# Attention and experts on one core: matrices fetched in halves on SyncE's queue, products issued per quarter and bank, transposes in place, a new order

## The chip, the cores and the metric

One core of one Trainium2 chip runs the kernel. The metric is the device time of one execution in microseconds (us). Engine names are those of the profile: PE is TensorE (PEld its weight loads), DVE is VectorE, ACT is ScalarE, POOL is GpSimd, SP is SyncE, which here only issues transfers. SPq and ACTq are the instruction streams that issue transfers from SyncE and ScalarE.

## The reference

For x of shape 4 x 11456 x 128 and 32 inducing points of 128 numbers, two attention blocks run one after the other, then a layer of 8 experts of which each token uses one.

```python
def mab(q, kv):
    s = scale * (q @ kv.transpose(0, 2, 1))
    s = s - s.max(-1, keepdims=True)
    a = np.exp(s)
    a /= a.sum(-1, keepdims=True) + 1e-09
    return a @ kv
h = mab(I, x)                      # 32 rows per batch
y = mab(x, h)                      # 11456 rows per batch
...
logits = y @ w_gate                # 8 experts
expert_idx = np.argmax(logits, axis=1)
probs = softmax(logits)
gate_w = probs[np.arange(N), expert_idx]
for e in range(E):                 # rows with expert_idx == e
    out[mask] = gate_w[mask, None] * (np.maximum(xe @ w1[e], 0.0) @ w2[e])
```

All data is float32.

## The kernel before

**Tiles.** Each of the 4 batches is cut into 4 quarters of rows, and each quarter into 6 groups of 15 blocks of 32 rows. So there are 24 tiles (k = 6b + g); one is 960 KB, 128 channels by 15 blocks by 4 quarters by 32 rows, and needs one load, one output of the same size and often a second load.

**First attention (names in the plan: LT, S1, M1, E1, T1, H).** A tile is loaded (`load_xt`, L599). `scores` (L611) multiplies it by the inducing points, four products into 32 rows of a bank each. A maximum per pair of tiles (`max1` L614, `max_spread` L637, `max_fold` L643 with `columns` L575, `max_all` L648) and an exponential on ACT (L651) follow; DVE turns the result in 32 x 32 blocks (L654, into another buffer), and 15 products (`h_sum`, L664) sum it with the tile in its other layout. That layout is loaded (`load_xn`, L602) for 10 tiles and made by 15 transposes on PE (`turn`, L622) with copies out of PSUM (`turn_out`; `copy`, L630 on ACT, L632 on DVE) for 14.

**Per batch (names hT to h4, C in the tables).** After its 6 tiles a batch has its 32 rows of h (`h_turn`, `h_norm` L686 to 688, `h_center` L697 to 699). In the second attention all rows of a batch mix nearly the same h, so one expert is picked per batch (`gate_mm`, `pick` L708 to 712), and its row number is written to memory. `fetch` (L716, L717) reads the number into a register of the issuing engine and loads that expert's two matrices, 1 MB, into the one buffer `wt`: on ACT's queue for batches 0 to 2, on SP's for batch 3. `units` (L744) multiplies h by the first matrix, three DVE steps (L749, L753, L757/758) apply the relu, `second` (L766) multiplies by the second matrix, and after a fold the 32 finished rows stand in `h4`. A margin per batch (L785 to 826) bounds where this shortcut holds; a general part after the main one redoes rows outside it, of which there are none here.

**Second attention (S2, M2, E2, LG, LV, LS, PR, C, CT, SP, W, X, V, OUT).** In 6 rounds of 4 tiles: scores with h (L611 again), maximum (L831, L832), exponential (L835), gate logits of the round (L839, L844, L856 to 887, turned back in L891), `spread` of the gate weight over the rows (four products of 32 rows, L896), `weigh` (L899), and `experts` (L903): four products, one for each quarter q, each of 32 rows of `h4` by 480 columns into a bank of its own. Four copies (`evict`, L630/632) bring the banks to an output tile, and SP stores it (L605).

**Buffers.** 18 large slots hold tiles, turned tiles and outputs; 20 of 128 x 480 hold exponentials and gate values; the 8 banks of PSUM are shared by all.

**The order.** It is written by a planner that runs when the kernel is built: `make_plan` lists the operations with ranks (tables in `PLAN`), needs and assumed durations, and `schedule` simulates the engines and at each free moment takes the ready operation of lowest rank. STICK is added to the rank of a PE operation that changes between column-tiled (C), full (F) and row-tiled (R) products. A copy may go to ACT or DVE: DVE takes it only if ACT is busy for more than BEHIND ns. For a transfer it assumes a start 1000 ns after issue (START), 420 bytes per ns in all (RATE), shared by weight between the heads of the queues (7680 for SP's tiles, 8192 for the matrices), and 360 ns to land (LANDING); at most 2 transfers of SP are in flight in the plan. On the chip every engine runs its instructions in this order, each when its semaphores allow.

Of the kernel before, what the change touches and what calls it, by code (L numbers as in the profile page):

```python
# [31 lines left out]
NCONST = 128 + 128 + 4 + 8 + 1 + 12 + 64 + 4  # L32


HOP, SAME, FREE, START, LANDING, RATE = 70, 35, 40, 1000, 360, 420
SWITCH, STICK, INFLIGHT, BEHIND = 150, 315, 2, 66
# [11 lines left out]
class Op:  # L48
    __slots__ = ("name", "rank", "dur", "fn", "deps", "take", "use", "kind", "dma", "seq", "eng", "start", "end", "left", "ready", "param")

    def __init__(self, name, rank, dur, fn, deps=(), take=(), use=(), kind="", dma=None):
# [3 lines left out]
        self.eng = self.start = self.end = None  # L55
# [4 lines left out]
class Lines:  # L60
    def __init__(self):
        self.queues, self.at = {}, 0

    def put(self, o, when, queue, size, weight):
        self.queues.setdefault(queue, []).append([when, size, weight, o])

    def shares(self, t):
        heads = [q[0] for q in self.queues.values() if q and q[0][0] <= t]
        total = sum(h[2] for h in heads)
        return [(h, RATE * h[2] // total) for h in heads]  # L70
# [7 lines left out]
    def advance(self, t):  # L78
        landed = []
        while True:  # L80
# [4 lines left out]
            for q in self.queues.values():  # L85
                if q and q[0][0] <= n and q[0][1] <= 0:
                    landed.append((n, q.pop(0)[3]))
                    if q and q[0][0] < n:
                        q[0][0] = n
        self.flow(t)  # L90
# [8 lines left out]
def schedule(ops, caps, groups):  # L99
# [12 lines left out]
    busy = dict.fromkeys(ENGINES, 0)  # L112
    lines = Lines()
    events, order, done, t = [], [], 0, 0
    kind, pe_end, cold, inflight = "", 0, COLD, 0
# [37 lines left out]
    while done < len(ops):  # L153
        for e in ENGINES:
# [11 lines left out]
            o = best[2]  # L166
            for x in o.dur:
                ready[x].remove(o)
# [4 lines left out]
            if e == "PE":  # L173
                if t - pe_end > IDLE:
# [10 lines left out]
            if o.dma:  # L185
                inflight += e == "SP"
                lines.put(o, t + START, *o.dma)
# [8 lines left out]
        for when, o in lines.advance(t):  # L196
            inflight -= o.eng == "SP"
            o.end = when + LANDING
# [1053 lines left out]
```

## Time and profile before

| | |
|---|---|
| median of 3 runs | 195.26 us (195.07 to 195.92) |
| the profiled execution, its own time | 194.98 us |
| its span, first to last instruction | 192.9 us |
| mean granted TensorE clock | 0.917 |
| busy: PE, DVE, ACT | 155.9, 129.2, 94.5 us |
| moved | 61.88 MB, mean 321 GB/s |

The span is what the trace shows; 2.1 us of the execution's own time lie outside it. A line of a group of instructions gives line, engine, operation, output and input with their shapes, and the count; a helper such as `copy` or `columns` gives its own line to all who call it. A float32 product is recorded as two. The clock is a share of full speed (2.4 GHz); it has two levels, and a value between them is a mean over a stretch. "idle before" is how long the engine had nothing to run, with the instruction or transfer that ended it.

### The profile page before, as it was taken

Reading aid. Unit: us, or ns where it says so; the run is one execution under the profiler, and the core shown is the slowest. Engines: PE = TensorE matmul, PEld = TensorE weight load, DVE = VectorE, ACT = ScalarE, POOL = GpSimd, SP = SyncE. Lnnn points to the kernel's source line nnn. Section 1 sums busy time; section 2 is a strip of 40 time slices with the busy share of each in tenths; the row PEclk is TensorE's granted clock in tenths of the full one; section 3 lists DMA queues with packets and bytes.
Section 4 is the critical chain, followed back from the end, with each engine's and each line's share of the span. In section 5 each row is a group of like instructions: output and inputs, shape, how many; then the busy total and the mean of one; then the engine's idle time right before and its main releaser. Section 6 shows DMA issues by size and latency. Waiting matters only on the chain.

```text
span 192.9 us, 5128 instructions
## 1 busy us (share of the span) xinstructions
PE 155.9 (81%) x2060; PEld 84.5 (44%) x2061; DVE 129.2 (67%) x357; ACT 94.5 (49%) x193; POOL 14.9 (8%) x78
## 2 busy tenths in 40 slices
PE   7569999698299999939999995698999489979500
PEld 6148558353157576334635321534652135624200
DVE  0163565489079899927879996279999739877600
ACT  3165553138133636915564957008686908652800
POOL 1000000020002202001300020001202000012000
PEclk9999999999879999987999999789999958975965
DMA  5999999999932903994999999960598896798990
GB/s 197 424 424 423 422 420 418 422 410 430 413 162 43 339 32 108 423 328 180 345 359 425 412 420 423 426 284 7 207 404 236 267 424 267 308 422 350 395 397 31
DMA packets 9389, 61.88 MB, mean 321 GB/s; under 512 B 1296, under 2 KB 1424, under 8 KB 8848
## 3 DMA queue, kind: packets, MB, share of 16 engines
q1 hardware_dynamic: 8640, 58.16, 76.0%
q10 hardware_dynamic: 720, 3.33, 4.2%
q8 instruction: 18, 0.29, 0.6%
q14 instruction: 11, 0.09, 0.1%
HBM read 37.89 MB, written 23.59 MB: 319 GB/s over the span
## 4 chain that ended last, share of the span: by engine, by line
PE 44%; DMA 30%; DVE 15%; issue 3%; ACTq 1%; SPq 0%; ACT 0%
DMA wt<-in_w 18%; DMA big<-in_xT 12%; PE bank L903 10%; PE bank L611 9%; PE bank L664 9%; PE bank L622 6%; PE bank L896 4%; DVE mid L899 3%; PE bank L839 2%; DVE big L632 2%; PE bank L575 2%; PE bank L744 2%; DVE mx L831 2%; DVE mid L654 2%; ACTq L716 1%
## 5 line engine op out<-in xcount | busy, mean ns | idle before, releaser
L630 ACT COPY big<-bank 128x480 f32<-128x480 f32 (+2 forms) x120 | 60.2, 570 | 56.7 <-PE bank L622 32.1
L903 PE MATMUL bank<-mid,h 32*128 32x480 f32 x192 | 34.4, 697 | 0.7 <-DVE mid L899 0.5
L611 PE MATMUL bank<-big,it_s 128*32 128x480 f32 x192 | 24.9, 578 | 4.3 <-DMA big<-in_xT 4.3
L622 PEld LDWEIGHTS bank<-csb,big 128*128 128x128 f32 x210 | 22.6, 141 | 12.7 <-issue 6.3
L622 PE MATMUL bank<-csb,big 128*128 128x128 f32 x210 | 27.3, 278 | 0.5 <-ACT mid L835 0.4
L664 PE MATMUL bank<-big,mid 128*32 128x129 f32 x720 | 25.9, 284 | 1.8 <-issue 1.7
L664 PEld LDWEIGHTS bank<-big,mid 128*32 128x32 f32 x720 | 22.7, 113 | 6.3 <-issue 3.2
L614 DVE TENSOR_REDUCE mx<-bank 128x1 f32<-128x480 f32 x24 | 15.5, 648 | 14.0 <-PE bank L611 13.7
L611 PE MATMUL bank<-big,hc 128*32 128x480 f32 x192 | 24.1, 589 | 0.3 <-ACT mid L835 0.3
L632 DVE COPY big<-bank 128x480 f32<-128x480 f32 (+2 forms) x32 | 20.1, 639 | 3.3 <-PE bank L622 1.9
L835 ACT ACTIVATE mid<-bank,nb 128x480 f32<-128x480 f32 x24 | 16.2, 674 | 12.0 <-DVE gzr L730 7.2
L903 PEld LDWEIGHTS bank<-mid,h 32*128 32x128 f32 x192 | 13.8, 210 | 16.1 <-ACT big L630 5.8
L651 ACT ACTIVATE mid<-bank,mx 128x480 f32<-128x480 f32 x24 | 15.3, 664 | 6.1 <-DVE mx L648 6.1
L654 DVE STREAM_TRANSPOSE mid<-mid 128x480 f32<-128x480 f32 x24 | 15.6, 661 | 1.5 <-ACT mid L651 1.5
L899 DVE TENSOR_TENSOR mid<-mid,bank 128x480 f32<-128x480 f32 x24 | 14.5, 643 | 2.6 <-PE bank L896 2.6
L831 DVE TENSOR_REDUCE mx<-bank 128x1 f32<-128x480 f32 x24 | 15.3, 638 | 1.2 <-PE bank L611 1.2
L744 PE MATMUL bank<-wt,hT_all 128*32 128x256 f32 x32 | 3.4, 508 | 14.5 <-DMA wt<-in_w 14.5
L749 DVE STREAM_TRANSPOSE gT<-bank 128x256 f32<-128x256 f32 x4 | 1.8, 450 | 14.9 <-PE bank L744 14.9
L896 PE MATMUL bank<-mid,sel 32*128 32x480 f32 x48 | 10.0, 743 | 1.4 <-DVE u L796 1.4
L611 PEld LDWEIGHTS bank<-big,it_s 128*32 128x32 f32 x192 | 5.3, 112 | 11.8 <-issue 4.3
L744 PEld LDWEIGHTS bank<-wt,hT_all 128*32 128x32 f32 x32 | 0.8, 124 | 17.2 <-issue 17.2
L611 PEld LDWEIGHTS bank<-big,hc 128*32 128x32 f32 x192 | 5.0, 113 | 7.7 <-issue 4.4
(95 smaller groups left out, 126.8 us busy)
## 6 DMA issues: line engine op xcount, KB each, us to landing
big<-in_xT SPq DMA_DIRECT2D x24, 960.0 KB, 11.6
out<-big SPq DMA_DIRECT2D x24, 960.0 KB, 6.1
big<-in_xn SPq DMA_DIRECT2D x10, 967.5 KB, 10.6
wt<-in_w ACTq DMA_DIRECT2D x3, 1024.0 KB, 9.0
wt<-in_w SPq DMA_DIRECT2D x1, 1024.0 KB, 6.6
csb<-in_consts ACTq DMA_DIRECT2D x1, 174.5 KB, 2.5
it_s<-in_indT SPq DMA_DIRECT2D x1, 16.0 KB, 2.3
wg_sb<-in_wg ACTq DMA_DIRECT2D x1, 4.0 KB, 5.3
```

The costliest lines, as they stand in the source:

```text
L611: self.nc.tensor.matmul(self.blk(ps[32 * q : 32 * q + 32, :GW]), lhsT=lhsT, rhs=x[:, :, q, :], start=True, stop=True)
L614: self.nc.vector.tensor_reduce(self.mx1[b][g // 2][:, g % 2 : g % 2 + 1], self.bank(fe)[:, :GW], AX.X, ALU.max)
L622: self.nc.tensor.transpose(ps[:, k * P : (k + 1) * P], x[:, k0 + k].rearrange("p q t -> p (q t)"), self.ident)
L630: self.nc.scalar.copy(dst, src)
L632: self.nc.vector.tensor_copy(dst, src)
L654: self.nc.vector.transpose(self.at(t), self.at(e))
L664: self.nc.tensor.matmul(ps[32 * j : 32 * j + 32, : P + 1], lhsT=e[:, k, :], rhs=x[:, k, :], start=(n < 4), stop=(n >= 2 * GB - 4))
L831: self.nc.vector.tensor_reduce(t, self.bank(fe)[:, :GW], AX.X, ALU.max)
L835: self.nc.scalar.activation(self.at(e), self.bank(fe)[:, :GW], AF.Exp, bias=self.nb2[k])
L896: self.nc.tensor.matmul(self.bank(s)[:, :GW], lhsT=self.sel[rows], rhs=self.at(ct)[rows], start=True, stop=True)
L899: self.nc.vector.tensor_tensor(out=self.at(e), in0=self.at(e), in1=self.bank(s)[:, :GW], op=ALU.mult)
L903: self.nc.tensor.matmul(self.bank(os_[q])[:, :GW], lhsT=self.h4[b][32 * q : 32 * q + 32, :], rhs=self.at(e)[32 * q : 32 * q + 32, :], star ...
```

## The change

- **Fetch.** All four fetches are issued by SP, each as two transfers of 512 KB: the first matrix, then the second. `units` waits for the first alone, `second` for the other too. The plan assumes 2600 ns to start and 600 to land for the first half.
- **Products.** `spread` and `experts` become one operation per tile and per quarter, each taking its own bank; the planner keeps a time for each of the four row tiles and waits for all of them when the kind changes. STICK is 7156 instead of 315, BEHIND 1821 instead of 66.
- **Copies.** Lists bind 57 copies of turned tiles and outputs to ACT and 42 to DVE.
- **Buffers.** DVE's transposes and the gate steps work in place, so 18 middle buffers do instead of 20, and there are 19 large slots instead of 18. `max_fold` writes to unused columns of the scores' bank. Several small buffers exist once or twice instead of four times.
- **Small steps.** `h_norm` sums as it multiplies; `pick` reads PSUM itself and a separate copy (`gate_out`) brings out the gate values; `max2` is cut into its two instructions; the warm-up is 3 products of 384 columns instead of 36 of 128; the inducing points and the gate matrix lie in the constants.
- **Order.** All ranks are new (numbers left out here).

```diff
...
-HOP, SAME, FREE, START, LANDING, RATE = 70, 35, 40, 1000, 360, 420
-SWITCH, STICK, INFLIGHT, BEHIND = 150, 315, 2, 66
+HOP, SAME, FREE, RATE, PAUSE, AGAIN, FIRST = 70, 35, 40, 420, 1500, 600, 330000
+SWITCH, STICK, INFLIGHT, BEHIND = 150, 7156, 2, 1821
...
+            if e == "PE":
+                clear = tiles[o.tile] if o.tile is not None and o.kind == kind else max(tiles)
+                if clear > t:
+                    busy[e] = clear
+                    heapq.heappush(events, (clear, 4, o.seq))
+                    continue
...
+                run = occ if o.tile is None else lat - 250
+                if t - max(tiles) > IDLE:
                     cold = max(cold, t + WINDOW)
                 if t < cold:
-                    occ, lat = 2 * occ, lat + occ
+                    occ, run, lat = 2 * occ, 2 * run, lat + run
                 if o.kind != kind:
-                    occ, lat = occ + SWITCH, lat + SWITCH
-                kind, pe_end = o.kind, t + occ
+                    occ, run, lat = occ + SWITCH, run + SWITCH, lat + SWITCH
+                kind = o.kind
+                if o.tile is None:
+                    tiles = [t + run] * 4
+                else:
+                    tiles[o.tile] = t + run
...
-SPW = 4
+JOIN = 1
+FETCH = ("SP", "SP", "SP", "SP")
 CAPS = {"gate": 2, "w": 1}
-GROUPS = {"mid": (20, {"e1": 5, "e1t": 4, "e2": 9, "lv": 2, "ls": 2, "ct": 3}), "bank": (8, {"fe": 4, "o": 5, "mi": 4, "sp": 4}), "big": (18, {"xt": 14, "xn": 5, "ob": 4})}
+GROUPS = {"mid": (18, {"e1": 6, "e2": 13, "lv": 4}), "bank": (8, {"fe": 6, "o": 8, "mi": 3, "sp": 3}), "big": (19, {"xt": 17, "xn": 6, "ob": 6})}
...
+    "ACT": [
+        "TE0.2", "TE10.1", "TE10.2", "TE12.1", "TE12.2", "TE13.1", "TE14.1", "TE14.3", "TE15.3", "TE16.1", "TE16.2",
+        "TE2.0", "TE4.3", "TE7.1", "TE7.2", "TE8.0", "TE9.0", "TE9.1", "TE9.2", "V0.0", "V0.1", "V0.3", "V1.0",
+        "V1.2", "V1.3", "V10.3", "V11.0", "V11.1", "V12.0", "V12.2", "V13.0", "V13.1", "V13.2", "V14.0", "V14.1",
+        "V15.1", "V15.2", "V15.3", "V17.0", "V18.0", "V18.1", "V19.0", "V19.3", "V2.3", "V20.0", "V22.0", "V3.1",
+        "V3.2", "V4.0", "V5.3", "V6.2", "V6.3", "V7.0", "V8.1", "V8.3", "V9.2", "V9.3", "h41", "h42", "h43",
+    ],
+    "DVE": [
+        "PC0", "PC2", "TE0.0", "TE0.3", "TE10.0", "TE10.3", "TE13.0", "TE13.2", "TE13.3", "TE14.0", "TE14.2",
+        "TE15.0", "TE15.1", "TE15.2", "TE16.3", "TE18.1", "TE18.2", "TE2.1", "TE2.2", "TE4.1", "TE4.2", "TE6.0",
+        "TE6.1", "TE6.3", "TE7.0", "TE8.1", "TE9.3", "V14.2", "V16.3", "V17.2", "V18.2", "V19.2", "V2.1", "V20.2",
+        "V21.0", "V21.2", "V21.3", "V22.1", "V22.2", "V22.3", "V23.0", "V23.2", "V3.0", "V8.0", "cc0", "h40",
+    ],
...
+        if name in side:
+            e = side[name]
+            dur, fn = {e: dur[e]}, lambda f=fn, e=e: f(e)
...
-                    tt = last = op(f"T1.{ku}", ("A", ku, "T1"), {"DVE": (590, 655)}, lambda e=e1_, t=e1t_: K.turn_e(e, t), [ex], take=[e1t_], use=[e1_])
+                    tt = last = op(f"T1.{ku}", ("A", ku, "T1"), {"DVE": (590, 655)}, lambda e=e1_: K.turn_e(e), [ex], use=[e1_])
                     if u == NG - 1:
...
-        a = hT = op(f"hn{b}", ("C", b, "hn"), vec(840), lambda mi=m0, b=b: K.h_norm(mi, b), [a], use=[m0])
-        a = hc = op(f"hc{b}", ("C", b, "hc"), vec(560), lambda b=b: K.h_center(b), [a])
+        a = hT = op(f"hn{b}", ("C", b, "hn"), vec(910), lambda mi=m0, b=b: K.h_norm(mi, b), [a], use=[m0])
+        a = hc = op(f"hc{b}", ("C", b, "hc"), vec(380), lambda b=b: K.h_center(b), [a])
         m0 = Buf("mi")
         a = op(f"cg{b}", ("C", b, "cg"), pe(400), lambda mi=m0, b=b: K.gate_mm(mi, b), [hc], take=[m0], kind="C")
-        a = ix = op(f"ix{b}", ("C", b, "ix"), vec(900), lambda mi=m0, b=b: K.pick(mi, b), [a], use=[m0])
+        a = ix = op(f"ix{b}", ("C", b, "ix"), vec(740), lambda mi=m0, b=b: K.pick(mi, b), [a], use=[m0])
+        cc = op(f"cc{b}", ("C", b, "gt"), {"ACT": (185, 290), "DVE": (150, 240)}, lambda e, mi=m0, b=b: K.gate_out(e, mi, b), [a], use=[m0])
         w = Buf("w")
-        if b < B - 1:
-            ga = op(f"GA{b}", ("C", b, "GA"), {"ACT": (1100, 1100)}, lambda w=w, b=b: K.fetch("ACT", w, b), [ix], take=[w], dma=("ACT", 1048576, 8192))
+        if FETCH[b] == "ACT":
+            ga = gc = op(f"GA{b}", ("C", b, "GA"), {"ACT": (1300, 1300)}, lambda w=w, b=b: K.fetch("ACT", w, b, 0, 2 * F), [ix], take=[w], dma=("ACT", 1048576, 8192, 1950, 750))
         else:
-            ga = op(f"GA{b}", ("C", b, "GA"), {"SP": (1100, 1100)}, lambda w=w, b=b: K.fetch("SP", w, b), [ix], take=[w], dma=("SP", 1048576, 8192))
-        gz = op(f"gt{b}", ("C", b, "gt"), {"POOL": (550, 600)}, lambda b=b: K.gate_turn(b), [ix])
+            ga = op(f"GA{b}", ("C", b, "GA"), {"SP": (2000, 2000)}, lambda w=w, b=b: K.fetch("SP", w, b, 0, F), [ix], take=[w], dma=("SP", 524288, 4096, 2600, 600))
+            gc = op(f"GB{b}", ("C", b, "GA"), {"SP": (450, 450)}, lambda w=w, b=b: K.fetch("SP", w, b, F, 2 * F), [ga], use=[w], dma=("SP", 524288, 4096, 1000, 600))
+        gz = op(f"gt{b}", ("C", b, "gt"), {"POOL": (550, 600)}, lambda b=b: K.gate_turn(b), [ix, cc])
...
-        a = op(f"P{b}", ("C", b, "P"), pe(430), lambda mi=m0, w=w, b=b: K.second(mi, w, b), [gl], take=[m0], use=[w], kind="C")
+        a = op(f"P{b}", ("C", b, "P"), pe(430), lambda mi=m0, w=w, b=b: K.second(mi, w, b), [gl, gc], take=[m0], use=[w], kind="C")
...
-        for u0 in range(0, n, SPW):
-            us = list(range(u0, min(u0 + SPW, n)))
-            sps = [Buf("sp") for _ in us]
-            sp = op(f"SP{ks[u0]}", ("X", ks[u0], "SP"), pe(800), lambda sps=sps, ct=ct, us=us: K.spread(sps, ct, us), [cb], take=sps, use=[ct], kind="R")
-            for u, s in zip(us, sps):
-                k, b = ks[u], bs[u]
-                ob = Buf("ob")
-                wg = op(f"W{k}", ("X", k, "W"), {"DVE": (570, 660)}, lambda s=s, e=e2[u]: K.weigh(s, e), [sp], use=[s, e2[u]])
-                os_ = [Buf("o") for _ in range(NQ)]
-                x = op(f"X{k}", ("X", k, "X"), pe(800), lambda os_=os_, e=e2[u], b=b: K.experts(os_, e, b), [wg, h4s[b]], take=[*os_, ob], use=[e2[u]], kind="R")
-                vs = []
-                for q in range(NQ):
-                    vs.append(op(f"V{k}.{q}", ("X", k, "V"), {"ACT": act(480), "DVE": dve(480)}, lambda e, o=os_[q], ob=ob, q=q: K.evict(e, o, ob, q), [x], use=[os_[q], ob]))
-                op(f"OUT{k}", ("X", k, "OUT"), {"SP": (400, 400)}, lambda ob=ob, b=b, g=k % NG: K.store(ob, b, g), vs, use=[ob], dma=("SP", BYTES, 7680))
+        for u, (k, b) in enumerate(zip(ks, bs)):
+            s, ob, os_ = Buf("sp"), Buf("ob"), [Buf("o") for _ in range(NQ)]
+            sp = op(f"SP{k}", ("X", k, "SP"), {"PE": (40, 1050)}, lambda s=s, lv=lv, u=u: K.spread(s, lv, u), [cb], take=[s], use=[lv], kind="R", tile=u)
+            wg = op(f"W{k}", ("X", k, "W"), {"DVE": (570, 660)}, lambda s=s, e=e2[u]: K.weigh(s, e), [sp], use=[s, e2[u]])
+            vs, x = [], None
+            for q in range(NQ):
+                x = op(f"X{k}.{q}", ("X", k, "X"), {"PE": (40, 1050)}, lambda o=os_[q], e=e2[u], b=b, q=q: K.experts(o, e, b, q), [wg, h4s[b], x], take=[os_[q]] if q else [os_[q], ob], use=[e2[u]], kind="R", tile=q)
+                vs.append(op(f"V{k}.{q}", ("X", k, "V"), {"ACT": act(480), "DVE": dve(480)}, lambda e, o=os_[q], ob=ob, q=q: K.evict(e, o, ob, q), [x], use=[os_[q], ob]))
+            op(f"OUT{k}", ("X", k, "OUT"), {"SP": (400, 400)}, lambda ob=ob, b=b, g=k % NG: K.store(ob, b, g), vs, use=[ob], dma=("SP", BYTES, 7680, 1000, 360))
...
-        self.load = [lambda: nc.sync.dma_start(self.it_s, indT), lambda: nc.scalar.dma_start(csb, consts), lambda: nc.scalar.dma_start(self.wg, wg)]
+        self.load = lambda: nc.scalar.dma_start(csb, consts)
...
-        for i in range(9):
-            self.columns(self.bank(mi)[:, 0:P], self.ones, self.ones)
+        for i in range(3):
+            self.nc.tensor.matmul(self.bank(mi)[:, 0:384], lhsT=self.ones, rhs=self.ones.unsqueeze(1).to_broadcast([P, 3, P]), start=True, stop=True)
...
-    def turn_e(self, e, t):
-        self.nc.vector.transpose(self.at(t), self.at(e))
-
-    def zero_pad(self, t):
-        self.nc.gpsimd.memset(self.at(t)[64:128, (GB - 1) * 32 : GB * 32], 0.0)
...
+    def gate_out(self, e, mi, b):
+        self.copy(e, self.cg[b], self.bank(mi)[:, E : 2 * E])
+
+    def fetch(self, e, w, b, lo, hi):
         engine = self.nc.scalar if e == "ACT" else self.nc.sync
-        row = engine.value_load(self.ii[b][0:1, 0:1], min_val=0, max_val=(E - 1) * P)
-        engine.dma_start(self.wt[w.slot], self.w[bass.ds(row, P), :])
+        if lo == 0:
+            self.row = engine.value_load(self.ii[b][0:1, 0:1], min_val=0, max_val=(E - 1) * P)
+        engine.dma_start(self.wt[w.slot][:, lo:hi], self.w[bass.ds(self.row, P), lo:hi])
 
...
-    def spread(self, sps, ct, us):
-        for s, u in zip(sps, us):
-            rows = slice(32 * u, 32 * u + 32)
-            self.nc.tensor.matmul(self.bank(s)[:, :GW], lhsT=self.sel[rows], rhs=self.at(ct)[rows], start=True, stop=True)
+        self.nc.vector.transpose(self.lv3(lv, n), c)
+
+    def spread(self, s, lv, u):
+        rows = slice(32 * u, 32 * u + 32)
+        self.nc.tensor.matmul(self.bank(s)[:, :GW], lhsT=self.sel[rows], rhs=self.at(lv)[rows], start=True, stop=True)
...
-    def experts(self, os_, e, b):
-        for q in range(NQ):
-            self.nc.tensor.matmul(
-                self.bank(os_[q])[:, :GW],
-                lhsT=self.h4[b][32 * q : 32 * q + 32, :],
-                rhs=self.at(e)[32 * q : 32 * q + 32, :],
-                start=True,
-                stop=True,
-            )
+    def experts(self, o, e, b, q):
+        rows = slice(32 * q, 32 * q + 32)
+        self.nc.tensor.matmul(self.bank(o)[:, :GW], lhsT=self.h4[b][rows], rhs=self.at(e)[rows], start=True, stop=True)
...
```

## Rows read from the trace of the kernel before

**Rows 1.** The page: busy us (share) xinstructions; GB/s in 40 slices of the span.
```profile
PE 155.9 (81%) x2060; PEld 84.5 (44%) x2061; DVE 129.2 (67%) x357; ACT 94.5 (49%) x193; POOL 14.9 (8%) x78
GB/s 197 424 424 423 422 420 418 422 410 430 413 162 43 339 32 108 423 328 180 345 359 425 412 420 423 426 284 7 207 404 236 267 424 267 308 422 350 395 397 31
```

**Rows 2.** Stretches: length, busy us (x) of each engine, clock, transfer share, GB/s.
```profile
52.03:55.60 3.57, 3.57 (x24) 1.10 (x24) 1.26 (x3) 0.00 (x0) 0.00 (x0) 0.58 0.79 325
55.60:80.00 24.40, 24.25 (x376) 15.99 (x376) 22.57 (x66) 13.59 (x29) 3.68 (x18) 1.00 0.44 154
...
84.90:89.50 4.60, 4.59 (x54) 2.27 (x58) 2.32 (x7) 0.59 (x2) 0.60 (x3) 0.63 0.84 314
...
122.15:127.10 4.95, 4.95 (x76) 3.36 (x76) 2.19 (x7) 0.00 (x0) 0.00 (x0) 0.66 1.01 420
127.10:150.60 23.50, 22.37 (x340) 10.51 (x336) 22.63 (x65) 15.64 (x34) 3.29 (x14) 1.00 0.56 206
...
154.85:162.00 7.15, 7.15 (x37) 3.21 (x38) 4.65 (x13) 2.45 (x6) 0.28 (x2) 0.58 0.80 335
...
170.00:183.70 13.70, 9.71 (x52) 3.97 (x50) 9.26 (x23) 6.68 (x14) 1.69 (x8) 0.75 0.94 388
183.70:192.90 9.20, 0.00 (x0) 0.00 (x0) 0.00 (x0) 0.00 (x0) 0.00 (x0) 0.56 0.52 207
```

**Rows 3.** Waits for L744: us in total, times, longest; timeline, first and last.
```profile
PE bank L744 <- DMA wt<-in_w: 14.5, 4, 4.7
...
52.03 1.08 PE L744 MATMUL bank<-wt,hT_all 128*32 128x256 f32 x8 [4.69 <-DMA wt<-in_w]
...
154.85 1.08 PE L744 MATMUL bank<-wt,hT_all 128*32 128x256 f32 x8 [3.05 <-DMA wt<-in_w]
```

**Rows 4.** The chain: start, us, what; then landings of the four fetches.
```profile
40.40 0.17 DVE ii L712
...
41.52 10.38 DMA wt<-in_w
...
146.31 0.16 DVE ii L712
...
148.14 6.58 DMA wt<-in_w
...
DMA to landing us min/median/max: 6.6/9.0/10.4
```

**Rows 5.** Issues on SP's queue, KB, median us to landing; landings of L605's stores.
```profile
big<-in_xT SPq DMA_DIRECT2D x24, 960.0 KB, 11.6
...
DMA to landing us min/median/max: 3.7/6.1/12.8
```

**Rows 6.** Timeline of PE around a row-tiled product: start, us, instructions.
```profile
109.98 0.99 PE L611 MATMUL bank<-big,it_s 128*32 128x480 f32 x8
...
110.79 0.99 PE L611 MATMUL bank<-big,hc 128*32 128x480 f32 x8
...
111.71 1.09 PE L903 MATMUL bank<-mid,h 32*128 32x480 f32 x8
...
112.72 1.01 PE L611 MATMUL bank<-big,hc 128*32 128x480 f32 x8
```

**Rows 7.** Timeline: one product that waited within itself, and four in a row.
```profile
116.04 1.62 PE L903 MATMUL bank<-mid,h 32*128 32x480 f32 x8
...
164.70 5.42 PE L903 MATMUL bank<-mid,h 32*128 32x480 f32 x32
```

**Rows 8.** Page, groups: copies out of PSUM to large tiles.
```profile
L630 ACT COPY big<-bank 128x480 f32<-128x480 f32 (+2 forms) x120 | 60.2, 570 | 56.7 <-PE bank L622 32.1
...
L632 DVE COPY big<-bank 128x480 f32<-128x480 f32 (+2 forms) x32 | 20.1, 639 | 3.3 <-PE bank L622 1.9
```

**Rows 9.** Timeline of SP: its first transfer.
```profile
0.77 0.39 SPq L513 DMA_DIRECT2D it_s<-in_indT  x1
```

More of the change, by code (lines that the diff above doesn't have):

```diff
@@ L48, with __init__ @@
 class Op:
-    __slots__ = ("name", "rank", "dur", "fn", "deps", "take", "use", "kind", "dma", "seq", "eng", "start", "end", "left", "ready", "param")
-    def __init__(self, name, rank, dur, fn, deps=(), take=(), use=(), kind="", dma=None):
+    __slots__ = ("name", "rank", "dur", "fn", "deps", "take", "use", "kind", "dma", "seq", "eng", "start", "end", "left", "ready", "param", "tile")
+    def __init__(self, name, rank, dur, fn, deps=(), take=(), use=(), kind="", dma=None, tile=None):
         self.name, self.rank, self.dur, self.fn = name, rank, dur, fn
@@ L61, in __init__, with put @@
     def __init__(self):
-        self.queues, self.at = {}, 0
-    def put(self, o, when, queue, size, weight):
-        self.queues.setdefault(queue, []).append([when, size, weight, o])
+        self.queues, self.at, self.last = {"SP": [[1000, FIRST, 7680, None, True]]}, 0, 0
+    def put(self, o, when):
+        queue, size, weight, start, _ = o.dma
+        q, when = self.queues.setdefault(queue, []), when + start
+        if queue == "SP" and not q and when - self.last > PAUSE:
+            when += AGAIN
+        q.append([when, size, weight, o, queue == "SP"])
     def shares(self, t):
-        heads = [q[0] for q in self.queues.values() if q and q[0][0] <= t]
+        heads = [q[0] for q in self.queues.values() if q and q[0][0] <= t and q[0][4]]
         total = sum(h[2] for h in heads)
@@ L89, in advance @@
                         q[0][0] = n
+                    if name == "SP":
+                        edge, self.last = True, n
+            sp = self.queues["SP"]
+            if edge or not sp or sp[0][0] > n:
+                for q in self.queues.values():
+                    if q and q[0][0] <= n:
+                        q[0][4] = True
         self.flow(t)
@@ L112, in schedule @@
     busy = dict.fromkeys(ENGINES, 0)
+    busy["SP"] = 10
     lines = Lines()
-    events, order, done, t = [], [], 0, 0
-    kind, pe_end, cold, inflight = "", 0, COLD, 0
+    events, order, done, t = [(10, 2, 0)], [], 0, 0
+    kind, tiles, cold, inflight = "", [0] * 4, COLD, 0
     def fits(o):
@@ L774, in part_out @@
     def part_out(self, e, mi, b):
-        self.copy(e, self.part[b], self.bank(mi)[:, 0:P])
+        self.copy(e, self.part[0], self.bank(mi)[:, 0:P])
     def part_fold(self, mi, b):
-        self.columns(self.bank(mi)[:, 0:P], self.fold, self.part[b])
+        self.columns(self.bank(mi)[:, 0:P], self.fold, self.part[0])
     def h4_out(self, e, mi, b):
@@ L934, in attn_moe_kernel @@
                 o.fn()
-    general_part(tc, K, xT, wg, w, out)
+    general_part(tc, K, xT, w, out)
 def blk(t):
```

210 lines of the change are left out of this document (112 added, 98 removed), and 177 rows, old and new, of the table PLAN.

## The prediction

> **What bounds the kernel now.** I began with the page's busy shares: TensorE 81% and VectorE 67% of a span of 192.9 us, with the memory traffic at up to 424 GB/s but nearly nothing in some slices [rows 1]. A mean hides where the time goes, so next came busy time and clock by stretch [rows 2]. TensorE is busy without a break in 55.6 to 80, while the transfers run at 0.44 of their share; in 127.1 to 150.6 it works 22.4 of 23.5 us at a transfer share of 0.56. In the middle of the kernel it is the order and speed of TensorE that counts, with VectorE close behind (22.6 of 24.4 and 22.6 of 23.5 us). What breaks this up is seen in the list of waits: four times TensorE stands before the product with the picked expert's first matrix (L744) for its load, 14.5 us together, 4.69 the first and 3.05 the last time [rows 3]. Behind every one of these waits the granted clock is low: 0.58, 0.63, 0.66 and 0.58 as means of stretches of 3.57, 4.60, 4.95 and 7.15 us [rows 2], a mixture of the full 2.4 GHz with the lower level, 1.2 GHz. Length times the missing share is 1.5 + 1.7 + 1.7 + 3.0 = 7.9 us. Waits and clock together: 22.4 us.
>
> **Why TensorE arrives too early.** The order is written by a planner in the kernel that assumes when a fetch lands. In the old code that is 1.0 us after the index is ready, plus the transfer (1 MB at 8192/15872 of 420 GB/s beside SyncE's queue, 4.84 us), plus 0.36: 6.2 us. The chain shows the truth for b=0: index ready at 40.57, landing at 41.52 + 10.38 = 51.90, so 11.3 us [rows 4]. That is 5.1 more than assumed, and TensorE waited 4.69 [rows 3]. For b=3, on SyncE's queue, it took from 146.47 to 154.72, 8.25 us, against 3.9 assumed with nothing ahead: 4.4 more, wait 3.05. The waits are the planner's error, less some slack.
>
> **Part by part.**
>
> *Fetch in halves on SyncE's queue, new due times.* The new code counts 2.6 us to start, 0.5 MB at 420 GB/s (1.25) and 0.6: 4.45 us, plus what the queue holds ahead. From rows: index to issue on SyncE was 1.67 us (146.47 to 148.14) [rows 4]; the quickest 960 KB store landed in 3.7 us [rows 5], of which half its 2.32 us at 424 GB/s falls away: 2.6; so 4.3 from below. From above, the b=3 fetch landed in 6.58 with a store ahead; less 1.24, plus 1.67: 7.0. I take a value near the lower end, 0.75 us over the plan each time, since the plan counts transfers ahead by itself: 3.0 of the 14.5 us stay, **-11.5 us**. Ends: all 14.5 gone; or, with as much ahead as the median load has (11.6 us to landing [rows 5], so 11.6 - 1.24 + 1.67 = 12.0, against 4.45 + two transfers of 2.32 = 9.1 planned), 2.9 us each, only -2.8. The second half is needed only after three VectorE steps on the first product; cover gone, it costs its own 1.24 us. The index read now stands at the head of SyncE's queue, so loads and stores behind it are held for that 1.67 us four times. While loads land 11.6 us after their issue several are already out, and from 55.6 to 80 the lines are half idle; I count nothing, and 6.7 us if every one of them were short.
>
> *Clock.* With waits of under 1 us the stretch behind should mostly stay at 2.4 GHz. Not all: the kernel's last working stretch, 170 to 183.7, has 0.75 with no fetch near [rows 2]. Ends 0 and -7.9; I take two thirds, **-5 us**.
>
> *Products by quarter.* The same 96 quarter products and 24 spreads run, but something may now stand between quarters. Each visit from column tiles to row tiles and back has a price in the rows: two column products start 0.81 apart, a row product 0.92 after one, and the next column product 1.01 after that [rows 6]; 0.92 + 1.01 - 2 x 0.81 = 0.31 us. Six of 24 groups broken once: **+1.9 us**. From below, the four starved products that took 5.42 us [rows 7] instead of 4 x 1.01 give back 1.4. The end above is a rival.
>
> The Trainium skill (TensorEngine Tiling (Array Packing), Key Properties) says that a change of tiling mode drains the engine, which speaks against breaking groups. The 0.31 us agree. By the rule alone, with all 24 groups broken once at that price, this term would be 7.4 us and the sum 185.6 instead of 180.1; one mode held across groups would make it nothing.
>
> *Copies bound to engines.* The new lists bind 42 copies out of PSUM (25 of turned tiles, 17 of outputs) to VectorE, where 32 ran, and the large BEHIND keeps the free ones on ScalarE: 110 there instead of 120. VectorE gets 10 x 0.639 = 6.4 us more, ScalarE 5.7 less [rows 8]. VectorE then has about 135.6 us; at the 92% that it reaches in 55.6 to 80 that is 147 us, plus 9.2 us after the last copy [rows 2]: 156 before the start is counted. That doesn't set a time near 180, but leaves little under 170. I count 0.
>
> *The rest.* The 16 KB load ahead of the first data load (0.39 us of issue [rows 9]) goes: **-0.3**; nothing if the first load was not late by it. The matrix columns ride with the constants, 20 KB more on ScalarE's queue, covered by the first load's flight. The warm-up in three wider products, the maximum's fold in a spare corner of a bank, the extra small copy of the gate, the halved maximum step, the transpose in place: same work or small steps off the long chains, 0; if in-place transposes were slower, VectorE's slack in the old gaps pays. The 19th large slot lets one more load start early; lines are half idle when slots bind, so 0, and at best one transfer, 2.3 us. The new order itself I can't read from the table of ranks; -4 to +4 around 0, the size of one of the old waits.
>
> **Sum.** The profiled execution took 194.98 us (span 192.9 and 2.1 around it), 0.28 under the median of 195.26. 194.98 - 11.5 - 5 + 1.9 - 0.3 = 180.1; with the 0.28, **180.4 us**. Own range 175 to 187: from the ends near each term and the order's 4 us.
>
> **Rivals.**
>
> *Everything hides (172 us).* Waits and clock loss all go: 195.26 - 14.5 - 7.9 - 0.3 = 172.6. For it: TensorE-bound stretches have work in reserve. Against: at b=3 little other work is left, and VectorE is 92 to 96% busy in the dense stretches.
>
> *The queue eats the gain (194 us).* On SyncE's queue the fetch stands behind what was issued before. With the median load's 11.6 us, -2.8, +1.9 and -0.3 leave 194.1, and the clock loss stays. For it: the median load waits that long, and a store up to 12.8 [rows 5]. Against: the order of the queue is the plan's, and the b=3 fetch landed in 6.58 there.
>
> The Trainium skill (DMA: Bandwidth & Descriptors, Queues, rings and completion order) has each engine take turns between queue rows packet by packet. By that rule a fetch on a row of its own gets its share at once, and moving it onto SyncE's row trades this for a place in line. The trace has a median landing of 9.0 us over all four and 6.6 for the one on SyncE's queue [rows 4], and doesn't settle it.
>
> *Quarters fall apart (200 us), the one on the slow side.* A product whose quarters run in pairs takes two passes of 0.81 us, 1.62, as one starved product did [rows 7], and a visit costs 0.31: +0.92 for each of 24 is 22 us. 195.26 - 16.8 + 22 = 200.5. It decides from 16.8/24 = 0.70 us per product on: a mean of 1.71 instead of 1.01. For it: one bank is now enough to start a quarter, so banks freed one by one start lone quarters. Against: the planner's price for a switch (STICK from 315 to 7156) now holds it to a kind, and its model knows the four row tiles.
>
> **Chances.** Forecast 0.50; everything hides 0.17; the queue eats the gain 0.15, in which about 0.07 stays faster, 0.06 within and 0.02 slower; quarters fall apart 0.18. Faster by over 0.5% (about what a measurement here can tell from no change): 0.74; within: 0.06; slower: 0.20. The range 171 to 196 takes in the forecast, most of the first rival and the queue; some 0.03 below and 0.17 above are left out.
>
> **What would show it.** Right: waits of TensorE for the expert matrix under 5 us in total, first halves landing within 7 us of issue, mean granted clock over 0.94 (0.917 before), VectorE near 136 us busy and ScalarE near 89, product groups (lines of the expert product) still near 1.01 us when banks are free. Wrong: a list of waits in which the same load still costs over 10 us (queue), or many lone quarter products with column products between, TensorE busy time above 160 us (quarters), or loads held behind SyncE's index read while the lines are idle.

## The result and the profile after

| | before | after |
|---|---|---|
| median us | 195.16 (193.63 to 195.92, 4 runs) | 174.58 (173.12 to 175.52, 4 runs) |
| profiled execution, span us | 194.98, 192.9 | 174.46, 172.7 |
| mean granted clock | 0.917 | 0.971 |

The ratio is 0.895 with an interval of 0.887 to 0.903: 20.6 us less, where 14.9 were forecast. A second series of the kernel after, on another chip beside experiments 9 and 10, had a median of 175.57 us (174.62 to 176.22). Runs of the kernel before differ by up to 7 us on one chip, with the clock granted to each (192.14 us at 0.934, 199.15 at 0.893), so the experiments give the difference of the fastest runs beside that of the medians; here it is 20.5.

The page of the kernel after, the lines of [rows 1] with that of the clock in 40 slices:

```profile
PE 147.7 (86%) x1994; PEld 82.0 (48%) x1995; DVE 132.4 (77%) x367; ACT 89.8 (52%) x183; POOL 15.1 (9%) x78
PEclk9999999999999999999999999999999999999855
GB/s 161 419 427 427 422 427 428 416 417 417 413 424 423 388 391 67 390 390 400 352 377 174 331 401 386 234 233 388 294 258 260 390 428 425 420 425 429 418 414 59
```

The span splits into TensorE's busy and idle time: 155.9 + 37.0 us became 147.7 + 25.0. So 12.0 us of the gain are idle time that went, and 8.2 are busy time, the net of several terms that are taken apart below. The transfers hardly stop now: one slice is under 100 GB/s ahead of the last, where [rows 1] has three.

The waits for the first matrix, which answer to [rows 3] (total, times, longest):

```profile
PE bank L820 <- DMA wt<-in_w: 1.3, 1, 1.3
```

The landings of all eight halves, which answer to [rows 4]:

```profile
DMA to landing us min/median/max: 4.7/7.1/9.4
```

Three of the four products with the first matrix on the timeline (start, us):

```profile
64.61 0.64 PE L820 MATMUL bank<-wt,hT_all 128*32 128x256 f32 x8
...
112.39 0.64 PE L820 MATMUL bank<-wt,hT_all 128*32 128x256 f32 x8 [1.25 <-DMA wt<-in_w]
138.81 0.64 PE L820 MATMUL bank<-wt,hT_all 128*32 128x256 f32 x8
```

14.5 us of waits have become 1.3. Three of the four products no longer wait at all. Each takes 0.64 us instead of the 1.08 that [rows 3] show at the lower clock. The chain of the one that still waits (start, us):

```profile
104.87 0.16 DVE ii L784
...
106.08 6.17 DMA wt<-in_w
```

From the index (105.03) to the landing (112.25) it is 7.2 us, where [rows 4] has 11.3 for b=0. With the others it is the order that covers the landing. For b=0 the index is ready at 46.40, but SyncE first issues a load that stands ahead and has no slot before 51.11; the fetch goes out at 52.49 and TensorE, at other work all the way, reaches the product at 64.61, 12 us later.

How the stretches of [rows 2] end now (columns as there):

```profile
155.00:160.00 5.00, 4.49 (x32) 2.68 (x24) 5.00 (x10) 3.54 (x7) 0.00 (x0) 1.00 1.02 424
162.00:172.70 10.70, 0.15 (x2) 0.07 (x1) 0.16 (x1) 0.00 (x0) 0.00 (x0) 0.54 0.67 271
```

TensorE has the full clock up to the end of its work, where [rows 2] has 0.58 and 0.75. The last 10.7 us are nearly stores alone, as the last 9.2 us were before.

The copies, which answer to [rows 8], and the products by quarter (busy us, mean ns):

```profile
L699 ACT COPY big<-bank 128x480 f32<-128x480 f32 (+2 forms) x110 | 55.2, 574 | 38.6 <-PE bank L691 21.9
L982 PE MATMUL bank<-mid,h 32*128 32x480 f32 x192 | 30.9, 607 | 0.9 <-DVE mid L978 0.7
L701 DVE COPY big<-bank 128x512 f32<-128x512 f32 (+2 forms) x42 | 26.1, 646 | 4.5 <-PE bank L691 4.2
...
L975 PE MATMUL bank<-mid,sel 32*128 32x480 f32 x48 | 14.5, 603 | 0.5 <-DVE mid L971 0.5
```

110 and 42 copies, as forecast. Four quarters of a product, eight records, still run as one pass where they stand together, as here between two sets of scores (timeline):

```profile
116.10 1.39 PE L680 MATMUL bank<-big,hc 128*32 128x480 f32 x12
117.42 1.09 PE L982 MATMUL bank<-mid,h 32*128 32x480 f32 x8
118.44 0.32 PE L733 MATMUL bank<-big,mid 128*32 128x129 f32 x4
```

In the order of the instructions 22 of the 24 products have their four quarters side by side; two have one quarter apart. The spreads (L975) did not keep together: in five of the six rounds their four quarters are issued in two or more parts, as here, three of them and the fourth 8.6 us later:

```profile
106.04 2.20 PE L975 MATMUL bank<-mid,sel 32*128 32x480 f32 x6
...
114.68 1.07 PE L975 MATMUL bank<-mid,sel 32*128 32x480 f32 x2
```

### The profile page after: what moved, and what is told of

The parts are those of the page before. It is cut to its first block, busy times and chain, and to the rows that moved or that the text cites. A ratio compares the mean times of both kernels' runs of the same rounds, so it can differ in the third digit from the quotient of the medians.

```text
span 172.7 us, 5018 instructions
## 1 busy us (share of the span) xinstructions
PE 147.7 (86%) x1994; PEld 82.0 (48%) x1995; DVE 132.4 (77%) x367; ACT 89.8 (52%) x183; POOL 15.1 (9%) x78
## 4 chain that ended last, share of the span: by engine, by line
PE 54%; DMA 30%; DVE 4%; issue 3%; ACT 2%; SPq 0%; DVEq 0%
DMA big<-in_xT 16%; PE bank L680 14%; PE bank L982 12%; PE bank L733 9%; PE bank L691 8%; DMA big<-in_xn 4%; PE bank L975 4%; DMA wt<-in_w 4%; DMA csb<-in_consts 3%; DMA out<-big 3%; DVE big L701 2%; PE bank L919 2%; PE bank L644 2%; ACT big L699 2%; PE bank L820 1%
## 5 line engine op out<-in xcount | busy, mean ns | idle before, releaser
L699 ACT COPY big<-bank 128x480 f32<-128x480 f32 (+2 forms) x110 | 55.2, 574 | 38.6 <-PE bank L691 21.9
L982 PE MATMUL bank<-mid,h 32*128 32x480 f32 x192 | 30.9, 607 | 0.9 <-DVE mid L978 0.7
L701 DVE COPY big<-bank 128x512 f32<-128x512 f32 (+2 forms) x42 | 26.1, 646 | 4.5 <-PE bank L691 4.2
L680 PE MATMUL bank<-big,csb 128*32 128x480 f32 x192 | 24.3, 570 | 4.0 <-DMA big<-in_xT 2.7
L733 PE MATMUL bank<-big,mid 128*32 128x129 f32 x720 | 24.2, 274 | 3.5 <-DMA big<-in_xn 2.2
L683 DVE TENSOR_REDUCE mx<-bank 128x1 f32<-128x480 f32 x24 | 15.5, 647 | 11.7 <-PE bank L680 11.3
L915 ACT ACTIVATE mid<-bank,nb 128x480 f32<-128x480 f32 x24 | 15.8, 676 | 12.5 <-DVE nb L910 10.7
L720 ACT ACTIVATE mid<-bank,mx 128x480 f32<-128x480 f32 x24 | 15.2, 661 | 11.3 <-DVE mx L717 11.1
L982 PEld LDWEIGHTS bank<-mid,h 32*128 32x128 f32 x192 | 12.7, 183 | 14.5 <-ACT big L699 4.7
L975 PE MATMUL bank<-mid,sel 32*128 32x480 f32 x48 | 14.5, 603 | 0.5 <-DVE mid L971 0.5
L680 PEld LDWEIGHTS bank<-big,csb 128*32 128x32 f32 x192 | 5.8, 109 | 10.5 <-issue 5.9
L975 PEld LDWEIGHTS bank<-mid,sel 32*128 32x128 f32 x48 | 4.6, 183 | 5.1 <-ACT big L699 2.2
L919 PE MATMUL bank<-mid,gzb 128*32 128x480 f32 x48 | 6.0, 574 | 0.0
L902 POOL COPY thr_all<-thr 32x1 f32<-32x1 f32 x24 | 4.3, 177 | 19.5 <-DVE thr L895 18.7
```

Source lines behind the costliest of these rows:

```text
L680: self.nc.tensor.matmul(self.blk(ps[32 * q : 32 * q + 32, :GW]), lhsT=lhsT, rhs=x[:, :, q, :], start=True, stop=True)
L683: self.nc.vector.tensor_reduce(self.mx1[b][g // 2][:, g % 2 : g % 2 + 1], self.bank(fe)[:, :GW], AX.X, ALU.max)
L699: self.nc.scalar.copy(dst, src)
L701: self.nc.vector.tensor_copy(dst, src)
L720: self.nc.scalar.activation(self.at(e), self.bank(fe)[:, :GW], AF.Exp, bias=self.mx1[b][p + 1][:, 2:3], scale=SCALE)
L733: self.nc.tensor.matmul(ps[32 * j : 32 * j + 32, : P + 1], lhsT=e[:, k, :], rhs=x[:, k, :], start=(n < 4), stop=(n >= 2 * GB - 4))
```

## The experiments

Medians are of four runs, beside seven runs of the kernel before on the same chip: 196.22 us (192.14 to 199.15) for the first four, 194.54 (192.29 to 198.2) for the next four, 194.72 (190.98 to 196.18) for the last two. "Order kept" means that each engine runs its instructions in the order of the kernel named; the planner had no part in the edit.

**1. Known rows, in the order of before.** The expert's row is a constant here, so the choice of the expert isn't followed by the fetch; the fetch stands 6.5 us of the plan earlier on its old queue.

```diff
+        for b, e in enumerate(EXPERT):
...
+            order.insert(next(i for i, o in enumerate(order) if o.start >= ga.start - EARLY), ga)
...
+            ga.fn = lambda e=e, queue=queue: queue.dma_start(K.wt[0], K.w[e * P : e * P + P])
```

> The kernel before, its order kept, but the four fetches (still whole, on their old queues) take the expert's row as a constant and are issued about 6.5 us of the plan earlier, so each lands before TensorE comes to its product. Theory A (the gain is the wait for the expert matrix and the clock lost behind it, 14.5 + 7.9 us): no wait at that product, no half-clock stretches behind it, time 171 to 177 us, all of what the whole change brought. Theory B (the finer products, slots and new ranks bring much of it): the wait goes but new waits take its place, time 183 to 189 us.

Measured: 176.19 us (174.83 to 178.87), no wait for the matrix, clock 0.959. The page of this run:

```profile
PE 147.5 (85%) x2060; PEld 81.1 (47%) x2061; DVE 128.3 (74%) x357; ACT 94.7 (55%) x193; POOL 15.0 (9%) x78
...
PEclk9999999999999999999999969999999999999755
...
L904 PE MATMUL bank<-mid,h 32*128 32x480 f32 x192 | 30.5, 609 | 0.8 <-DVE mid L900 0.8
...
L897 PE MATMUL bank<-mid,sel 32*128 32x480 f32 x48 | 7.8, 612 | 1.7 <-DVE u L797 1.4
```

Its longest list entry among the waits of TensorE:

```profile
PE bank L612 <- DMA big<-in_xT: 6.9, 5, 3.0
```

With the old products, copies, buffers and order, taking the waits away is worth 20.0 us (17.3 between the fastest runs). TensorE is busy for 147.5 us, as after (147.7), though not a product was changed: the 8.4 us that went are clock. What is late next are tiles (6.9 us of waits, against 4.3 for this line in the kernel before), and behind the longest of these waits the clock is still low (timeline):

```profile
101.22 1.83 PE L612 MATMUL bank<-big,it_s 128*32 128x480 f32 x8 [2.96 <-DMA big<-in_xT]
102.79 1.84 PE L612 MATMUL bank<-big,hc 128*32 128x480 f32 x8
```

From 101.22 to 104.56 two products take 3.3 us, where two such at full clock take about 1.7 [rows 6]. Without this too, busy time would have fallen by about 10 us, an estimate from these rows.

**2. The wait filled with products that nobody reads.** Kernel before, order kept.

```diff
         ps = self.bank(mi)
+        for i in range(10):
+            self.columns(ps[:, 256:384], self.ones, self.ones)
```

> The kernel before with ten groups of small column products (128 columns, into the same bank, not read by anyone) issued just ahead of the product that waits for the expert matrix. The wait itself stays (about 14.5 us less some 2 to 3 us of fill each). If the clock behind the waits is a cost of its own (7.9 us in the profile), the granted clock behind them is over 0.9 and the time is 187 to 191 us. If other engines set the pace there anyway, the clock rises and the time stays at 194 to 196 us. If the fill outlasts the loads, it is slower than 196 us.

Measured: 188.31 us (187.84 to 189.37), so 7.9 less than before (4.3 between the fastest runs), by adding work; clock 0.955. The page of this run:

```profile
PE 160.1 (85%) x2380; PEld 90.7 (48%) x2381; DVE 128.9 (69%) x357; ACT 94.6 (50%) x193; POOL 15.0 (8%) x78
...
PEclk9999999999999999999999999799999999988955
```

The stretches behind the four waits and the last one (columns as in [rows 2]):

```profile
51.62:55.60 3.98, 3.98 (x41) 2.48 (x41) 2.86 (x7) 1.11 (x3) 0.00 (x0) 1.00 0.81 334
82.55:87.10 4.55, 4.19 (x70) 2.16 (x70) 2.55 (x8) 1.17 (x3) 0.56 (x3) 1.00 0.95 326
119.25:122.80 3.55, 3.55 (x60) 3.15 (x64) 1.39 (x4) 0.00 (x0) 0.00 (x0) 0.52 1.03 429
152.14:158.30 6.16, 5.62 (x44) 2.08 (x46) 4.89 (x13) 3.59 (x8) 0.48 (x2) 1.00 0.99 414
165.54:176.40 10.86, 8.55 (x51) 3.25 (x50) 8.47 (x22) 5.09 (x12) 1.70 (x8) 0.84 0.98 401
```

The loads come no sooner (6.8 to 10.1 us from issue to landing, against 6.6 to 10.4): behind the filler 5.8 us of waits are left. The filler itself takes 9.6 us; with the idle time of TensorE, 27.4, that is 37.0, as much as was idle before. So the 5.4 us by which this span (187.5) is shorter than that of before are the products, at a higher clock: the lower clock behind the waits was a cost of its own. Behind three of the four waits it is gone; behind the longest that is left (2.31 us) it isn't. Length times the missing share is 1.7 us behind the waits instead of 7.9, and 1.7 in the last stretch instead of 3.4.

**3. Fetch on SyncE's queue in halves, alone.** Kernel before, order kept.

```diff
-        engine = self.nc.scalar if e == "ACT" else self.nc.sync
+        engine = self.nc.sync
...
-        engine.dma_start(self.wt[w.slot], self.w[bass.ds(row, P), :])
+        engine.dma_start(self.wt[w.slot][:, 0:F], self.w[bass.ds(row, P), 0:F])
+        engine.dma_start(self.wt[w.slot][:, F : 2 * F], self.w[bass.ds(row, P), F : 2 * F])
```

> The kernel before, its order kept, with only the fetch changed: all four on SyncE's queue in two halves, each at the place in the order where the fetch stood. Theory A (the place of the product in TensorE's order counts, the queue and the halves bring a quarter of the gain at most): waits for the matrix 7 to 11 us in total instead of 14.5, time 186 to 191 us. Theory C (the earlier landing of the first half is the gain): waits under 4 us, time 173 to 180 us. Rival D (the place in line eats it): waits 14 us or more, time 194 to 198 us.

Measured: 181.32 us (180.91 to 182.72), clock 0.957. The waits for the matrix:

```profile
PE bank L745 <- DMA wt<-in_w: 4.3, 3, 1.5
```

This part alone brings 14.9 us (11.2 between the fastest runs), where the whole change brought 20.6; no wait is over 1.5 us, and the result lies between theories A and C. The waits for tiles (L611) grew, from 4.3 to 8.2 us.

**4. The kernel after with whole fetches on ScalarE's queue,** in its own order, at the place of the first half.

```diff
+            if o.name[:2] == "GA":
+                K.fetch("ACT", o.take[0], int(o.name[2]), 0, 2 * F)
+                continue
+            if o.name[:2] == "GB":
+                continue
```

> The kernel after, its order kept, with only the fetch undone: one load of both matrices on ScalarE's queue, at the place in the order where the first half was issued. Theory A: TensorE has other work until the load lands for batches 0 and 1; batches 2 and 3 wait some 3 to 5 and 1 to 2 us; time 178 to 182 us. Theory C: waits for the matrix of 10 us or more and half-clock stretches behind them, time 188 us or more.

Measured: 180.58 us (176.81 to 182.44). The waits:

```profile
PE bank L820 <- DMA wt<-in_w: 5.3, 3, 2.5
```

The longest on the timeline:

```profile
67.45 1.01 PE L820 MATMUL bank<-wt,hT_all 128*32 128x256 f32 x8 [2.51 <-DMA wt<-in_w]
```

So the other parts without the new fetch bring about as much as the fetch without the other parts, 15.6 us against 14.9 (15.3 against 11.2 between the fastest runs), and both together 20.6. They overlap because both take from the same 22 us.

**5 and 6. The two halves of that edit apart,** kernel before, order kept: whole fetches, all on SyncE's queue (the first two lines of the diff of experiment 3), and halves on the old queues (its last three).

> The kernel before, its order kept; all four fetches on SyncE's queue but whole, one load of both matrices. With halves there the waits for the matrix were 4.3 us in total and the time 181.3 us. Theory Q (it is the queue: in line on SyncE's queue a load has the lines to itself): each whole load lands 1.2 to 1.7 us after where the first half did, waits 9 to 11 us, time 184 to 188 us. Theory H (it is the halving: TensorE needs only the first matrix): waits 13 us or more, time 191 us or more.

> The kernel before, its order kept; the fetches on their old queues (ScalarE's for batches 0 to 2, SyncE's for 3), but each in two halves. Theory H: a first half that shares the lines lands 2.5 us or more before the whole did (9.0 us), waits 4 to 7 us, time 181 to 186 us. Theory Q: sharing keeps the first half as late as the whole, waits 11 us or more, time 190 us or more.

Measured: 184.5 us (183.34 to 185.65) and 185.18 (184.89 to 186.03); ratios 0.952 (0.941 to 0.963) and 0.956 (0.947 to 0.965). Waits and landings of the whole fetches on SyncE's queue:

```profile
PE bank L744 <- DMA wt<-in_w: 7.3, 3, 2.9
...
DMA to landing us min/median/max: 4.9/6.9/10.9
```

The same views of the halves on the old queues:

```profile
PE bank L745 <- DMA wt<-in_w: 8.1, 4, 2.9
...
DMA to landing us min/median/max: 4.8/8.7/12.1
```

Each step alone brings about 10 us (9.0 and 7.4 between the fastest runs) and both 14.9 (experiment 3 was on another chip). Neither theory holds alone: the times fit Q in experiment 5 and H in experiment 6, the waits fit neither, and on ScalarE's queue the first halves landed in 8.2 to 9.1 us, not 2.5 us before the whole.

The median of 6.9 us against 9.0 [rows 4] doesn't show that a place in line is quicker than a queue of its own. Of the three fetches that moved, two landed sooner than before (4.9 and 7.4 us against 10.4 and 8.9) and one later (10.9 against 9.0). The quickest met no line: from 31.9 us on SyncE stood before the index read, and issued none of the loads behind it before the index was there (timeline of SP, and a stretch as in [rows 2]):

```profile
26.20 5.67 SPq L599 DMA_DIRECT2D big<-in_xT  x2
41.97 0.35 SPq L717 DMA_DIRECT2D wt<-in_w  x1
42.42 26.68 SPq L599 DMA_DIRECT2D big<-in_xT  x8
...
42.00:44.00 2.00, 2.00 (x28) 1.12 (x30) 1.95 (x5) 1.91 (x4) 0.35 (x3) 1.00 0.40 90
```

In the kernel before SyncE issued three loads in this time. So the fetch went ahead of loads that were held back, and for 10 us, not the 1.67 us of the prediction. The fetch that landed late had two loads and a store issued in the 4.3 us ahead of it. In experiment 3 SyncE held loads back in the same way.

Neither run answers the sentence of the prediction that rests on the Trainium skill (DMA: Bandwidth & Descriptors, Queues, rings and completion order). Turns between rows are in keeping with the trace of the kernel before, in which ScalarE's queue (q10) and SyncE's (q1) shared the lines from 45 to 49 us (packets, MB, share):

```profile
q10 hardware_dynamic: 108, 0.88, 53.2%
q1 hardware_dynamic: 107, 0.75, 44.9%
```

That each engine takes turns packet by packet isn't visible in these sums.

**7. Each expert product broken once.** Kernel after, order kept; four narrow column products that nobody reads stand between the second and third quarter.

```diff
+        if q == 1:
+            self.columns(self.bank(o)[:, GW : GW + E], self.ones, self.ones[:, 0:E])
```

> The kernel after with one change: between the second and third quarter of each of the 24 expert products stand four column products of 8 columns, written to unused columns of that quarter's bank. This makes the break that the slow rival feared, once in every product. Price by the rows of before: 0.31 us a visit, 24 of them 7.4 us, plus the two passes instead of one (0.8 us each at most): TensorE busy 7 to 25 us more. If TensorE is the bound through the stretch of outputs: time 181 to 195 us. If the stores have become the bound there: under 178 us.

Measured: 185.57 us (184.49 to 186.35), 11.0 over the kernel after on another chip; ratio to before 0.955 (0.945 to 0.966). One product on the timeline:

```profile
120.39 1.07 PE L982 MATMUL bank<-mid,h 32*128 32x480 f32 x4
121.39 0.25 PE L644 MATMUL bank<-ones 128*32 128x8 f32 x8
121.57 1.07 PE L982 MATMUL bank<-mid,h 32*128 32x480 f32 x4
```

The page:

```profile
PE 165.2 (90%) x2186; PEld 87.9 (48%) x2187; DVE 133.4 (72%) x367; ACT 91.7 (50%) x183; POOL 15.0 (8%) x78
```

Two quarters take as long as four: 1.07 us, twice, where the whole product took 1.09. 17.5 us more busy time over 24 is 0.73 each, a little of it a stretch at a lower clock (0.57 from 78 to 82 us); in time it is 11.0 over 24, 0.46 each. The rival "quarters fall apart" put 0.92 on it: the price is real but smaller, and the kernel doesn't break its expert products. By the Trainium skill (TensorEngine Tiling (Array Packing), Key Properties) a change of mode drains the engine: the 0.31 us of a visit [rows 6] agree, and here the second pass, 1.07 us, is the larger part.

**8. Ten of VectorE's copies given back to ScalarE.** Kernel after, order kept.

```diff
+FLIP = ("TE2.1", "TE6.1", "TE8.1", "TE10.0", "TE13.2", "TE14.0", "TE15.1", "TE16.3", "V3.0", "V8.0")
...
+            dur, fn = {e: dur[e]}, lambda f=fn, e="ACT" if name in FLIP else e: f(e)
```

> The kernel after, its order kept, with 10 of the 42 copies that it binds to VectorE run on ScalarE instead (eight of turned tiles, two of outputs), so VectorE has 6.4 us less to do and ScalarE 5.7 more. Prediction's term (VectorE does not set the time): within 1 us of the kernel after, 173.5 to 175.5 us. If VectorE is the co-bound of the dense stretches: 169 to 172 us. If ScalarE has become one by it: over 176 us.

Measured: 175.3 us (173.42 to 176.99); the interval of its ratio, 0.890 to 0.912, overlaps that of the kernel after. The page:

```profile
PE 150.4 (86%) x1994; PEld 83.9 (48%) x1995; DVE 127.4 (73%) x357; ACT 94.6 (54%) x193; POOL 15.0 (9%) x78
```

VectorE has 5.0 us less to do and nothing is gained beyond the 3.6 us by which these runs differ: VectorE isn't the bound, and the split of the copies isn't where the time came from.

**9. True due times alone.** Kernel before; the planner is told of 4 us more before a fetch starts and writes a new order by the old ranks.

```diff
-                lines.put(o, t + START, *o.dma)
+                lines.put(o, t + START + (4000 if o.name[:2] == "GA" else 0), *o.dma)
```

> The kernel before; the planner alone is told that a fetch takes 4 us longer to start than it assumed, and writes a new order by its old ranks; queues, whole fetches, products and slots as before. Theory W (the waits were the fault of the due times, and an order that knows when the load lands cures them): waits for the expert matrix under 3 us in total, time 180 us or less, as for the new order with whole fetches on ScalarE's queue. Rival R (a true due time only moves the gap: without new ranks nothing stands ready to fill it, and TensorE waits for other things instead): waits for the expert matrix under 3 us, yet 188 us or more, with TensorE idle for over 30 us.

Measured: 200.06 us (196.18 to 205.46); the profile is of the run of 205.46. The clock on the page:

```profile
PEclk9999999999999999999995866699999555899855
```

TensorE's longest entry in the list of waits:

```profile
PE bank L611 <- DMA big<-in_xT: 10.1, 6, 4.6
```

The fastest runs differ the same way, 196.18 against 190.98. Of the waits for the matrix 0.3 us are left, yet the time is longer and TensorE idles for 38.6 us of a span of 203.4. The rival R holds: a true due time takes the gap out of one place, and with the old ranks it opens in another. A wait that is gone from the list is not yet a gain.

**10. Known rows in the kernel after,** the first halves 4 us of the plan earlier, the second ones at their old place in the order (the expectation speaks of both); again no index is read, so the choice isn't followed.

```diff
+            ga.fn = lambda e=e: K.nc.sync.dma_start(K.wt[0][:, 0:F], K.w[e * P : e * P + P, 0:F])
...
+            gb.fn = lambda e=e: K.nc.sync.dma_start(K.wt[0][:, F : 2 * F], K.w[e * P : e * P + P, F : 2 * F])
```

> The kernel after in its own order, with the row of each batch's expert a constant, so that no index is read, and both halves issued 4 us of the plan earlier. Theory D (the fetch is done as a cost in the kernel after; its 1.3 us of waits and the index reads on SyncE's queue hold up nothing else): 172 to 175 us, within 1.5% of the kernel after. Rival S (SyncE standing before the index read holds back loads and stores, which costs time elsewhere): 170 us or less.

> The kernel after unchanged, beside the two others on the same chip: 173 to 176 us, as a measure of how far chips and runs differ.

Measured: 173.06 us (171.84 to 174.62), beside 175.57 for the kernel after unchanged. 2.5 us, 1.4% (2.8 between the fastest runs), is what waiting for index and fetch still costs; of it the waits for the two matrices are 1.9 us in the profile of the kernel after and 2.3 in that of experiment 11. Theory D holds, at its edge.

Not tried, because the planner writes another order as soon as they change: the 19th large slot, the transposes in place, and ranks, STICK and BEHIND each by itself. What the new order is worth beyond the waits is bounded only by experiments 1 and 10: with known rows the old order takes 176.19 us and the new one 173.06, on different chips.

## Why the prediction was right, and where its terms were off

The forecast, 180.4 us, had the sign, the mechanism and a range (171 to 196) that holds the 174.58, but missed by 5.8 us, and its own range (175 to 187) just misses it. Step by step:

- **Waits, -11.5 us: right.** 14.5 became 1.3, and 0.6 came up before the second matrix (L842): -12.6. TensorE's idle time fell by 12.0 us in all; forecast, with the -0.3 of the rest, 11.8. The reason was half right: the first halves landed in 7.7, 9.0, 6.2 and 4.7 us, not all within 7, and the cure is as much the later place of the product as the earlier landing (experiments 3 and 4).
- **Clock, -5 us: the step that failed.** "I take two thirds" of 7.9, with the stretch 170 to 183.7 left out as one that would stay at 0.75. In the old order, without these waits, busy time fell by 8.4 us, and by about 10 if the one stretch that stayed low is added (experiment 1). The sum over [rows 2] was too short by that last stretch: 13.7 x 0.25 = 3.4 us more were missing there, and in the kernel after TensorE works at 1.00 until 160. Length times the missing share over all but the tail is 192.9 x 0.083 - 9.2 x 0.44 = 12.0 us before, and 172.7 x 0.029 - 10.7 x 0.46 = 0.1 after. Why the end no longer drops stays open: a wait of 1.42 us for VectorE ahead of it stands unchanged in experiments 1 and 2, and the stretch from there on is at 1.00 in the one and at 0.84 in the other.
- **Products by quarter, +1.9 us: too small, and in the wrong place.** The expert products cost nothing: 30.9 us busy against 30.5 in experiment 1, two of them broken. The spreads are what fell apart: 14.5 us against 7.8. Counted once where their records overlap, both together hold TensorE for 40.9 us, against 37.3 with the old products: +3.6. The price of a break was too low as well, 0.46 us in time and 0.73 in busy time, not 0.31 (experiment 7).
- **Copies, 0: right.** VectorE 132.4 us busy (135.6 forecast), ScalarE 89.8 (89); moving ten back changed nothing.
- **The rest and the new order, -0.3 and 0:** the order alone is not separable; with the old ranks a cure of the waits brought nothing (experiment 9). That busy time is 147.7 us beside the 147.5 of experiment 1 is a coincidence: 3.6 more for the spreads, 1.6 less for the stretch that stayed low there, and some 2 less elsewhere. Full products, the transposes, come in 11 stretches instead of 19, so the kind changes less often; that this is the 2 us is not shown.

Of the rivals, "everything hides" (172 us) was the nearest, 2.6 us away: waits and clock, 22.4 us together, were nearly all the gain there was. That all of it goes was given 0.17, above all because VectorE was 92 to 96% busy in the dense stretches; it wasn't the limit (experiment 8). "The queue eats the gain" is refuted by experiments 3 and 5, where the fetch on SyncE's queue made the kernel 9 to 15 us faster.

## What to carry to other kernels

Add to a wait in the middle of a kernel the clock that is lost behind it, over the whole kernel and its end as well: here 14.5 us of waits cost 17 to 20. When a planner's order arrives too early for a load, both cures, a load that lands sooner and other work put ahead, take from the same sum, so don't add them; and judge a new order by TensorE's total idle time, not by the one wait that is gone. Row-tiled products may be issued one by one at no cost as long as they stay side by side, as the expert products did; where a planner parts them, as it did with the spreads, count the extra passes. A queue that reads an index holds back what stands behind the read until the index is there: put the read where the index is nearly ready.

## What the runs showed of the hardware that was not expected

- Work that nobody reads, put into a wait, made the kernel 7.9 us faster (196.22 to 188.31; 4.3 between the fastest runs): idle time and filler together stayed at 37.0 us, and the products ran at a higher clock.
- A 1 MB load landed in 4.9 us where the index read ahead of it had held back the other loads of its queue, in 8.9 to 10.4 on a queue of its own beside a stream of loads, and in 10.9 behind other transfers.
- Half of a row-tiled product takes as long as the whole, 1.07 us and 1.09.
